# Dummy 64x64 matmuls behind the warm-up, and the retention stretches at other steps of a fused retention and feed-forward kernel

## The chip, the cores and the metric

The kernel runs on one core of one Trainium2 chip. The metric is the device time of one execution in microseconds (us), taken as the median of several runs. TensorE (PE in the profile) does the matmuls; weight loads into its array stand as PEld. VectorE is DVE, ScalarE is ACT, GpSimd is POOL, and SyncE (SP) issues nearly all DMAs.

## The reference

Two stages, one after the other. Shapes: 8 batches, 8 heads, 576 positions, 64 per head; then 4608 tokens, model width 512, inner width 2048.

```python
scores = scale * np.matmul(q, k.transpose(0, 1, 3, 2))
gamma = 1.0 - 2.0 ** (-5.0 - np.arange(H))
rel = pos[:, None] - pos[None, :]
Dmat = np.where(rel >= 0, gamma[:, None, None] ** rel[None], 0.0)
attn = np.matmul(scores * Dmat[None], v)
x = attn.transpose(0, 2, 1, 3).reshape(B * S, H * D)
h = x @ w_in
out = (h - np.tanh(h)) @ w_out
```

## The kernel before, in words

**Tiling.** The 576 positions are cut into nine chunks (n = 0 to 8) of 64. One chunk of all eight batches is a block of 512 tokens. For each block the retention gives x, `mm1(n, f)` computes the f-th of sixteen 128-row pieces of h, and `mm2(n, f)` adds that piece's part of the output into four PSUM banks. Each of mm1 and mm2 is 12 matmuls of 128x128 by 512: every operand is split into a high word and a low word, and three of the four products are kept. In `mm1` the high word of x meets the high word of the weight first, and the low word of the weight is used by the last four matmuls (the first block's f = 0 and 1 have an order of their own).

**Retention.** For each chunk and batch there are three kinds of 64x64 matmul: scores of the chunk, the update of a running state, and the output (`m_score`, `m_state`, `m_out`). They run four at a time on the quarters of the array, in stretches that stand between the large matmuls. `entry` (first two blocks, two batches a time) and `entry3` (later blocks, three stretches for a block: batches 0 and 1, then 2 to 4, then 5 to 7) each are one stretch: the outputs of the batches that are due, their state updates, and last the scores of the batches that follow. In the trace a 64x64 float32 matmul stands as two records.

**Parts of the program.** First a warm-up of bf16 matmuls on zeros (`busy`), then the eight batches of chunk 0 one by one (loop over j; six filler matmuls `busy(6, BLK)` stand in it). Then `seq`: mm1 for blocks 0 and 1, 32 steps k, while the weights are loaded and turned into two words, one piece a step (`unit`, `step`: four operations on DVE at L133, L155, L141, L143, a mask by two on ACT at L100 and L105, and the high word by ACT at L148; L155 makes the low word of the piece before). As no output weight is ready yet, h of these blocks is set aside: in `spill` (in HBM), and for ten pieces first in `home` tiles in SBUF. The stretches `entry` stand at the steps in `early`. Then `late`: mm2 for blocks 1 and 0, 32 steps k, with h fetched back four steps ahead (`fetch`), tanh applied two steps ahead (`resume`), and the words made one step ahead (`words`); the three stretches `entry3` for block 2 stand at three steps k, and four (or two) steps behind each, the q and k for the scores of the next stretch are loaded and scaled (`load_part(rest[0], 0)`, `prep` on POOL). Last the main loop for n = 2 to 8: mm1, mm2 of the piece before, and three stretches at three values of f.

**Order.** `in_order` keeps every engine's instructions in the order of the program, SP's DMA issues too. Who waits for whom follows from tiles: a tile with a `tag` takes one of the tag's slots, and it can be written only when the last instruction that reads the slot's former tile has run, wherever in the program that instruction stands. Tags `wo0` to `wo15` have one slot each and end as the output weights. Before that they hold other things: the first chunk's inputs `a{j}` lie in `wo{15-j}` and are read last by the state update `first_states(b)` that each `entry` carries (`2 * (p - 3)` in the loop, for two batches); the `home` tile of pieces 6 and 7 takes `wo13`, that of 8 and 9 `wo12`, of 11 and 12 `wo11`, of 13 and 14 `wo10`:

```python
home = {0: 7, 1: 7, 6: 13, 7: 13, 8: 12, 9: 12, 11: 11, 12: 11, 13: 10, 14: 10}
loaded[j] = const.tile([P, 3, 4, C], F32, tag=f"wo{NF - 1 - j}", name=f"a{j}")      # load_first
nc.scalar.copy(homes[home[f]][:, (f + 1) % 2 if f > 1 else f], hp)                  # mm1, ACT
```

`pace` makes the weight loads wait for the last copy that ACT made of an h. `scale_k` scales four slices of the first chunk's keys on ACT, `scale_v` the values of a pair of batches on ACT, `scale_q` the queries on DVE.

Of the kernel before, what the change touches and what calls it, by code (L numbers as in the profile page):

```python
# [9 lines left out]
F32 = mybir.dt.float32  # L10
# [7 lines left out]
B, H, S, D = 8, 8, 576, 64  # L18
NT, DM, DF = B * S, H * D, 2048
P = 128  # L20
NF = DF // P
NCC = DM // P
C = 64
NC = S // C
BLK = B * C
# [7 lines left out]
WARM = 24  # L33
# [35 lines left out]
def retention_ffn(ctx: ExitStack, tc: tile.TileContext, ins, out, spill):  # L69
# [5 lines left out]
    psp = ctx.enter_context(tc.tile_pool(name="psp", bufs=1, space=PSUM))  # L75
# [173 lines left out]
    def half(k):  # L249
        return slice(64 * k, 64 * k + 64)  # L250
# [3 lines left out]
    def m_score(j, sc):  # L254
        a = loaded[j]
        return [
            (sc[half(c), i], a[half(c), 1, i, :], a[half(c), 0, i, :], True, True) for i in range(4) for c in range(2)
        ]
# [23 lines left out]
    def run(same, other):  # L282

        while same or other:
            for ms in (same, other):
                for out_, w, x, start, stop in ms[:2]:
                    nc.tensor.matmul(out_, w, x, start=start, stop=stop)  # L287
                del ms[:2]
# [35 lines left out]
    def bank(name, tag):  # L324
        return psp.tile([P, 2, 4, D], F32, tag=tag, bufs=2 if tag == "h" else 1, name=name)
# [5 lines left out]
    def pair(what, j, bank):  # L331
        return what(j, bank[:, 0]) + what(j + 1, bank[:, 1])
# [13 lines left out]
    def entry3(j, later=None):  # L346


        c0, b = divmod(j, B)
        single, states = b > 0, c0 < NC - 1  # L350
        then = j + 2 + single
        o = bank(f"own{j}", "own")
        outs, scores = pair(m_out, j, o), []
        if single:
            two = bank(f"two{j + 2}", "new")
            run(m_score(j + 2, two[:, 1]), outs[:8])
            after_score(j + 2, two[:, 1:], 1)
            outs = outs[8:]
            if states:

                new = bank(f"new{j + 2}", "h")
                run(m_state(j + 2, new[:, 0]), outs[:8])
                outs = outs[8:]
                kept = pool.tile([P, 1, 4, D], F32, tag="cv", bufs=4, name=f"kept{j + 2}")
                nc.scalar.copy(kept, new[:, :1])
        if states:
            new = bank(f"new{j}", "h")
            run(pair(m_state, j, new), outs[:16])
            outs = outs[16:]
        if single:  # L370
            if not states:
                run([], outs)
            outs = m_out(j + 2, two[:, 0], True)
            if states:
                add_state(j, new)
            low = after_out(j, o, 2, False)
        if then < NI:
            sc = bank(f"s{then}", "h")
            scores = pair(m_score, then, sc)
        run(scores, outs)  # L380
        if not single:
            if states:
                add_state(j, new)
            low = after_out(j, o, 2, False)
        low()
        if then < NI:
            after_score(then, sc, 2)
        if single:
            if states:
                add_state(j + 2, kept, 1)  # L390
            after_out(j + 2, two[:, :1], 1)
        def follow():

            more = then % B > 0
            if then >= NI:
                return
            load_part(then, 1)
            prep(then, 1)
            if more:
                load_one(then + 2)  # L400
                prep(then + 2, 1, 1)
                prep(then + 2, 0, 1)
            if later is None:
                load_part(then + 2 + more, 0)
                prep(then + 2 + more, 0)
            else:

                later.append(then + 2 + more)

        if later is None:  # L410
            follow()
        return follow
# [126 lines left out]
    warm = const.tile([P, BLK], BF16, tag="wi15", name="warm")  # L539
    nc.vector.memset(warm, 0.0)  # L540

    wps = psp.tile([P, BLK], F32, tag="new", bufs=1, name="wps")

    def busy(n, cols):
        for _ in range(n):
            nc.tensor.matmul(wps[:, :cols], warm[:, :P], warm[:, :cols], start=True, stop=True)

    busy(WARM, 140)
    busy(8, BLK // 2)
    decay = const.tile([P, 4, C], F32, tag="wo7", name="decay")  # L550
    krows = [const.tile([P, 4, 4, D], F32, tag=f"wo{4 + t}", name=f"krows{t}") for t in range(2)]

# [37 lines left out]
    for j in range(B):  # L590
        o = psp.tile([P, 8, C], F32, tag=("o2", "o3", "own")[j % 3], bufs=1, name=f"own_first{j}")[:, :4]
        run(score_first(j + 2) if j < B - 2 else [], m_out(j, o))
        if j < B - 2:
            after_score(j + 2, firsts[j + 2].unsqueeze(1), 1)
            if 0 < j < 5:
                paced(lambda: upto("load", j + 1))
        if j == 4:
            nc.sync.dma_start(vtab, vtab_d)
            nc.sync.dma_start(krows[0], krows_d[0])
            load_pair(B)  # L600
            nc.sync.dma_start(mask, mask_d)
            upto("load", 7)
            load_pair(B + 2)
        if j == 3:
            busy(6, BLK)
        low = after_out(j, o.unsqueeze(1), 1, False)
        if j == 0:

            paced(lambda: load_paced(6))
        if j < 6:  # L610
            low()
        else:
            lows.append(low)
        if j == 0:
            paced(lambda: load_paced(7))
        if j < 4:
            step()
# [18 lines left out]

    seq = [(n, f) for n in range(2) for f in range(NF)]
    late = [(1, f) for f in turn] + [(0, f) for f in range(NF)]
    early = {5: 4, 8: 5, 10: 6, 14: 7}
    scales = {2: 4, 4: 5, 7: 6, 9: 7, 13: 8}  # L640
    first = 2 * B
    for k, (n, f) in enumerate(seq):
        last_two = k - (len(seq) - 2)
        if k in (2, 6):
            scale_k(k // 4)
        if k + 1 in early:
            scale_v(2 * early[k + 1])
        if last_two < 0:
            step()
        else:  # L650
            fetch(*late[2 + last_two])
        mm1(n, f, ("h", "o2", "h", "o3")[k % 4] if k < len(seq) - 4 else ("o2", "o3", "h", "h")[k % 4])
        if last_two < 0:
            step()
            if k < 24:
                step()
        if k in scales:
            scale_q(2 * scales[k])
        upto("load", k + (7 if k < 11 else 6))
        for at, j, t in ((2, 12, 0), (5, 14, 0), (6, 12, 1), (8, 14, 1)):  # L660
            if k == at:
                load_part(j, t)
        if k in (9, 10):
            load_part(first, k - 9)
        for f in [f for f in home if home[f] == (7, 13, 12, 11, 10)[k - NF]] if NF <= k < NF + 5 else []:
            nc.sync.dma_start(spill[0, f], homes[home[f]][:, (f + 1) % 2 if f > 1 else f])
        if k == 3:
            nc.sync.dma_start(krows[1], krows_d[1])
            behind(tc, pace[-1])
            sc = scores_of(3)  # L670
            ms, done = first_states(0, "new")
            run(pair(m_score, B, sc) + ms, [])
            after_score(B, sc, 2)
            done()
        if k in early:
            p = early[k]
            more = first_states(2 * (p - 3), f"o{(p + 1) % 2}") if p < B - 1 else None
            entry(2 * p, scores_of(p), more)
        if k == 14:
            load_part(first + 2, 0)  # L680
        if k == 26:
            prep(first, 1)
        if k == 28:
            prep(first + 2, 0)
    rest = []
    for k, (n, f) in enumerate(late):
        if k in (3, 16, 29):
            follow = entry3(first + (0, 2, 5)[(3, 16, 29).index(k)], rest)
        if 0 < k < len(late) - 1:
            words(*late[k + 1])  # L690
        if k < len(late) - 2:
            resume(*late[k + 2])
        if k + 4 < len(late):
            fetch(*late[k + 4])
        if k in (3, 16, 29):

            follow()
        if k in (7, 20, 31):
            load_part(rest[0], 0)
            prep(rest.pop(), 0)  # L700
        for _ in range(2 if k < 4 else 1):
            step()
        if k < len(late) - 1:
            mm2(n, f)

    todo = [late[-1]]
    for n in range(2, NC):
        for f in range(NF):
            mm1(n, f)
            todo.append((n, f))  # L710
            if len(todo) > 1 and (n, f) != (NC - 1, NF - 2):
                mm2(*todo.pop(0))
            if n + 1 < NC and f in (2, 6, 14):

                entry3((n + 1) * B + (0, 2, 5)[(2, 6, 14).index(f)])
                mm2(*todo.pop(0))
    mm2(NC - 1, NF - 1)
    in_order(tc)
# [56 lines left out]
```

## Time and profile before

| | |
|---|---|
| median of 3 runs | 882.81 us (882.1 to 883.89) |
| the profiled execution | 883.72 us |
| its span, first to last instruction | 881.9 us |
| mean granted TensorE clock | 0.997 |
| PE busy | 872.7 us |
| DVE busy | 367.3 us |
| ACT busy | 294.4 us |
| POOL busy | 69.4 us |

Busy time is the time in which an engine had at least one instruction at work. Matmuls overlap in the array, so the records of two neighbours overlap too; what counts is the distance between their starts. In a timeline row the columns are the start from the beginning of the span, the time that the merged group took, engine, line, operation, out<-in, shapes, count, and in brackets the idle time of the engine just before with what ended it.

### The profile page before, as it was taken

The page shows a single profiled execution, that of the slowest core. Times are in us where ns is not written, and L with a number is a line of the kernel's source. Part 1 is how long each engine was busy: PE and PEld are TensorE (multiplying, and loading weights), DVE is VectorE, ACT ScalarE, POOL GpSimd, SP SyncE. Part 2 cuts the span into 40 slices and gives each one's busy share as a digit, 9 for nine tenths or more (in the row PEclk, how much of TensorE's full clock was granted, in tenths as well). Part 3 has the DMA queues.
Part 4 walks back from the last instruction along what each step waited for, and adds up shares of the span by engine and source line. Part 5 has one row for each costly group of instructions (what it writes and reads, how often), then busy time and mean ns, then how long its engine had stood idle before and what let it go on. Part 6 is the DMA issues. An engine that isn't in the chain of part 4 may idle for free.

```text
span 881.9 us, 17730 instructions
## 1 busy us (share of the span) xinstructions
PE 872.7 (99%) x7846; PEld 724.3 (82%) x7846; DVE 367.3 (42%) x571; ACT 294.4 (33%) x525; POOL 69.4 (8%) x73
## 2 busy tenths in 40 slices
PE   7999999999999999999999999999999999999997
PEld 6888888888888888888888888888888888888886
DVE  5989876554332333323332433233232332232222
ACT  4887754443222222222222222222222222222222
POOL 0001001011110001101110111001110111000000
PEclk9999999999999999999999999999999999999999
DMA  8966945552410121203220141112120321002001
GB/s 307 374 237 220 367 154 167 142 164 77 116 49 30 49 68 55 78 1 97 73 79 1 50 119 50 30 47 62 62 78 1 97 73 48 1 2 48 1 1 48
DMA packets 37628, 82.06 MB, mean 93 GB/s; under 512 B 4144, under 2 KB 5296, under 8 KB 37552
## 3 DMA queue, kind: packets, MB, share of 16 engines
q1 hardware_dynamic: 37024, 80.02, 28.5%
q8 instruction: 61, 1.00, 0.5%
q10 hardware_dynamic: 528, 0.92, 0.3%
q14 instruction: 15, 0.12, 0.0%
HBM read 63.62 MB, written 17.30 MB: 92 GB/s over the span
## 4 chain that ended last, share of the span: by engine, by line
PE 98%; DMA 1%; ACT 0%; DVE 0%; SPq 0%; issue 0%
PE o L495 45%; PE h L430 45%; PE new L287 2%; PE s L287 2%; PE own L287 2%; PE two L287 1%; DMA rwi<-in_w_in_dram 1%; DMA a<-in_first_dram 1%; PE new_first L287 0%; PE own_first L287 0%; SPq L555 0%; ACT mi L100 0%; ACT xh L313 0%; ACT mi L105 0%; PE s_first L287 0%
## 5 line engine op out<-in xcount | busy, mean ns | idle before, releaser
L430 PE MATMUL h<-xh,wi 128*128 128x512 f32 x1152 | 302.8, 391 | 0.5 <-ACT xh L313 0.5
L495 PE MATMUL o<-wo,gh 128*128 128x512 f32 x1144 | 289.8, 391 | 0.0
L430 PEld LDWEIGHTS h<-xh,wi 128*128 128x128 f32 x1152 | 216.3, 188 | 46.3 <-ACT xh L313 0.7
L495 PEld LDWEIGHTS o<-wo,gh 128*128 128x128 f32 x1144 | 213.1, 188 | 45.0
L456 DVE TENSOR_TENSOR g<-h,g 128x512 f32<-128x512 f32 x114 | 78.8, 691 | 341.5 <-ACT g L455 341.4
L455 ACT ACTIVATE g<-h 128x512 f32<-128x512 f32 x114 | 68.2, 598 | 363.6 <-PE h L430 362.8
L495 PE MATMUL o<-wo,gl 128*128 128x512 f32 x572 | 157.2, 389 | 0.0
L430 PE MATMUL h<-xl,wi 128*128 128x512 f32 x576 | 154.2, 389 | 0.0
L430 PEld LDWEIGHTS h<-xl,wi 128*128 128x128 f32 x576 | 108.1, 188 | 22.6
L495 PEld LDWEIGHTS o<-wo,gl 128*128 128x128 f32 x572 | 107.4, 188 | 22.3
L458 DVE TENSOR_TENSOR gl<-g,gh 128x512 fp32r<-128x512 f32 x113 | 81.0, 717 | 77.6 <-ACT gh L457 72.8
L457 ACT CAST gh<-g 128x512 fp32r<-128x512 f32 x113 | 70.1, 621 | 86.0 <-DVE g L456 86.0
L237 POOL TENSOR_TENSOR vr<-vr,vtab 128x512 f32<-128x512 f32 x21 | 22.4, 1068 | 611.0 <-DMA vr<-in_qkv_dram 525.3
L287 PE MATMUL own<-qk,state 64*64 64x64 f32 x736 | 45.2, 221 | 0.0
L287 PE MATMUL own<-qk,vr 64*64 64x64 f32 x736 | 44.1, 218 | 0.0
L287 PEld LDWEIGHTS own<-qk,vr 64*64 64x64 f32 x736 | 36.8, 135 | 0.0
L287 PEld LDWEIGHTS own<-qk,state 64*64 64x64 f32 x736 | 36.7, 134 | 0.0
L478 DVE TENSOR_TENSOR gl<-s,gh 128x512 fp32r<-128x512 f32 x30 | 23.1, 770 | 24.2 <-PE o L495 13.6
L237 POOL TENSOR_TENSOR qk<-qk,qtab 128x512 f32<-128x512 f32 x20 | 28.4, 1421 | 53.5 <-DMA qk<-in_qkv_dram 53.5
L477 ACT CAST gh<-s 128x512 fp32r<-128x512 f32 x30 | 18.6, 621 | 30.0 <-PE o L495 17.3
L287 PE MATMUL s<-qk 64*64 64x64 f32 x736 | 25.5, 219 | 0.0
L313 ACT CAST xh<-own 128x512 fp32r<-128x512 f32 x25 | 14.7, 586 | 29.9 <-PE own L287 29.9
(85 smaller groups left out, 568.6 us busy)
## 6 DMA issues: line engine op xcount, KB each, us to landing
qk<-in_qkv_dram SPq DMA_DIRECT2D x23, 512.0 KB, 5.9
vr<-in_qkv_dram SPq DMA_DIRECT2D x23, 512.0 KB, 4.5
rwi<-in_w_in_dram SPq DMA_DIRECT2D x16, 512.0 KB, 5.4
rwo<-in_w_out_dram SPq DMA_DIRECT2D x16, 512.0 KB, 5.2
out_dram<-ob SPq DMA_DIRECT2D x61, 128.0 KB, 2.4
s<-spill_dram SPq DMA_DIRECT2D x30, 256.0 KB, 2.7
one<-in_qkv_dram SPq DMA_DIRECT2D x14, 512.0 KB, 5.4
spill_dram<-g SPq DMA_DIRECT2D x20, 256.0 KB, 4.3
```

The source lines that it names most:

```text
L237: nc.gpsimd.tensor_tensor(a, a, table, op=ALU.mult)
L287: nc.tensor.matmul(out_, w, x, start=start, stop=stop)
L313: nc.scalar.copy(xh, o)
L430: nc.tensor.matmul(hp, win[f][:, a, cc, :], x[:, cc, :], start=(k == 0), stop=(k == 3 * NCC - 1))
L455: nc.scalar.activation(g, h, AF.Tanh)
L456: nc.vector.tensor_tensor(g, h, g, op=ALU.subtract)
L457: nc.scalar.copy(gh, g)
L458: nc.vector.tensor_tensor(gl, g, gh.bitcast(F32), op=ALU.subtract)
L477: nc.scalar.copy(gh, g)
L478: nc.vector.tensor_tensor(gl, g, gh.bitcast(F32), op=ALU.subtract)
L495: nc.tensor.matmul(ops[n][t], g[:, t * P : (t + 1) * P], wout[f_][:, a, :], start=(f_ == first and k == 0), stop=(f_ == final and k == 2),)
```

## The change

It alters five things: the warm-up is shorter and has twenty 64x64 float32 matmuls on zeros behind it, in two banks; the six fillers stand one run sooner; and the stretches of 64x64 matmuls stand at other steps in the three parts. In `seq` the first three entries go from steps 5, 8, 10 to 7, 9, 12 (with their `scale_v`, which stands a step ahead) and the second `scale_k` from step 6 to 7. In `late` the stretches go from steps 3, 16, 29 to 16, 22, 28, and the loads behind them from 7, 20, 31 to 20, 26, 31. In the main loop they go from f = 2, 6, 14 to 2, 5, 13.

```diff
-    busy(WARM, 140)
-    busy(8, BLK // 2)
+    busy(WARM, 130)
+    busy(8, 208)
+
+    zeros = warm.bitcast(F32)[:, :C]
+    more = psp.tile([P, 8, C], F32, tag="own", bufs=1, name="wps_own")
+    some = wps.rearrange("p (n c) -> p n c", c=C)
+    run(
+        [(some[half(c), i], zeros[half(c)], zeros[half(c)], True, True) for i in range(6) for c in range(2)],
+        [(more[half(1 - c), i], zeros[half(c)], zeros[half(c)], True, True) for i in range(4) for c in range(2)],
+    )
...
-        if j == 3:
+        if j == 2:
             busy(6, BLK)
...
-    early = {5: 4, 8: 5, 10: 6, 14: 7}
+    early = {7: 4, 9: 5, 12: 6, 14: 7}
...
-        if k in (2, 6):
+        if k in (2, 7):
             scale_k(k // 4)
...
-        if k in (3, 16, 29):
-            follow = entry3(first + (0, 2, 5)[(3, 16, 29).index(k)], rest)
+        if k in (16, 22, 28):
+            follow = entry3(first + (0, 2, 5)[(16, 22, 28).index(k)], rest)
...
-        if k in (7, 20, 31):
+        if k in (20, 26, 31):
             load_part(rest[0], 0)
             prep(rest.pop(), 0)
...
-            if n + 1 < NC and f in (2, 6, 14):
-                entry3((n + 1) * B + (0, 2, 5)[(2, 6, 14).index(f)])
+            if n + 1 < NC and f in (2, 5, 13):
+                entry3((n + 1) * B + (0, 2, 5)[(2, 5, 13).index(f)])
```

More of the change, by code (lines that the diff above doesn't have):

```diff
@@ L694, in retention_ffn @@
             fetch(*late[k + 4])
-        if k in (3, 16, 29):
+        if k in (16, 22, 28):
             follow()
-        if k in (7, 20, 31):
+        if k in (20, 26, 31):
             load_part(rest[0], 0)
```

## The prediction, before the changed kernel was run

> **What bounds the kernel now.** I read the page first, then the waits of PE without the first 18 us, then the chain that ended last, then the stretches around each moved step.
>
> ```profile
> PE 872.7 (99%) x7846; PEld 724.3 (82%) x7846; DVE 367.3 (42%) x571; ACT 294.4 (33%) x525; POOL 69.4 (8%) x73
> PE h L430 <- ACT xh L313: 0.5, 1, 0.5
> 74.29 46.47 PE h L430 x204
> ```
>
> PE is busy for 99% of the span. From 18 us to the end its only wait is the one of 0.5 us shown (the one at 18 us itself). In the chain, 204 large matmuls in a row take 46.47 us, 0.228 us each, so 12 of them (one mm1 or mm2) take 2.73 us. The program is one unbroken row of matmuls: a stretch that moves without a wait costs and gains nothing, and a wait that appears on PE is lost in full. So each moved step is asked one thing: are its inputs there when PE arrives?
>
> The only time to be won lies ahead of 18 us and just behind it:
>
> ```profile
> 8.56 0.63 ACT mi L105
> 9.94 5.31 DMA a<-in_first_dram
> 18.03 12.35 PE h L430 x48
> ...
> 6.60:10.00 3.40, 2.13 (x91) 1.77 (x89) 1.79 (x5) 1.81 (x4) 0.00 (x0) 1.00 1.02 400
> 13.40:16.80 3.40, 1.78 (x70) 1.45 (x64) 1.79 (x5) 1.24 (x4) 0.00 (x0) 1.00 0.95 372
> 16.90:20.20 3.30, 2.83 (x19) 2.26 (x16) 2.76 (x8) 2.54 (x8) 0.00 (x0) 0.50 0.97 330
> ```
>
> The first three rows are of the chain, the others of busy time by stretch (the first figure behind the length is PE's, the last but two the granted clock). The chain into mm1 is ACT's mask of the first weight at 8.56, behind it a load of first inputs that is issued at 9.94 and lands at 15.25, then the last runs of the first chunk and their copy by ACT. PE's own pace is no link of it before 15 us. From 16.9 to 20.2 the clock is granted at 0.50. There 48 matmuls take 12.35 us where 48 x 0.228 = 10.94: the dip costs some 1.4 us at most.
>
> **The change, part by part.**
>
> *Warm-up, dummies, fillers.* 24 x 10 + 8 x 48 = 624 columns of 5408 go, and 20 matmuls (40 records) come.
>
> ```profile
> 1.19 4.69 PE L546 MATMUL wps<-warm 128*128 128x140 bf16 x32 [1.19 <-DVE warm L540]
> 5.81 1.03 PE L287 MATMUL s_first<-a 64*64 64x64 f32 x16
> ```
>
> 4.69 us x 624 / 5408 = 0.54 us saved. Sixteen records of one list take 0.8 us from first to last start there, so 24 records with 16 more beside them in the other list take about 1.2. The first scores start some 0.7 us later. The load issued at 9.94 covers it, for what it waited behind is ACT's mask at 8.56 and not PE; without that cover it would cost 0.7. The fillers add nothing, one run sooner: what is behind them still waits for the landing at 15.25. I take 0 for all of it; the ends are -1.4 (the clock dip goes) and +0.7.
>
> *`early`, 5 to 7.* This step meets a slot. `home` of piece 6 takes `wo13` at step 6. `a2` lies there, and its last reader is the state update in the first entry. Before, that entry stood at step 5. Now it stands at step 7, so the copy of piece 6 on ACT waits for a stretch that PE reaches only after mm1 of piece 7. ACT keeps its order, and behind that copy stand the mask, the high word of weight piece 8, the four slices of `scale_k` (now at 7), and the copy and high word of the next step.
>
> ```profile
> 37.99 0.27 PE L287 MATMUL s<-qk 64*64 64x64 f32 x2
> 39.91 1.10 PE L287 MATMUL new_first<-a,krows 64*64 64x64 f32 x32
> 40.94 1.19 PE L430 MATMUL h<-xh,wi 128*128 128x512 f32 x4
> ...
> 40.51 0.58 ACT L313 CAST xh<-own 128x512 fp32r<-128x512 f32 x1
> 41.54 1.71 ACT L630 ACTIVATE krows<-krows,vtab 128x256 f32<-128x256 f32 x4
> 43.99 0.59 ACT L435 COPY home<-h 128x512 f32<-128x512 f32 x1 [0.74 <-PE h L430]
> 45.73 0.60 ACT L148 CAST wi<-mi 128x512 fp32r<-128x512 f32 x1
> 46.24 1.28 ACT L247 ACTIVATE vr<-vr,vtab 128x128 f32<-128x128 f32 x4
> ...
> 41.12 0.69 DVE L315 TENSOR_TENSOR xl<-own,xh 128x512 fp32r<-128x512 f32 x1 [0.57 <-ACT xh L313]
> 45.86 0.69 DVE L133 SCALAR_TENSOR_TENSOR mi<-rwi,mi 128x512 int32<-128x512 int32 x1 [0.92 <-ACT mi L105]
> 46.47 0.68 DVE L155 TENSOR_TENSOR wi<-mi,wi 128x512 fp32r<-128x512 f32 x1
> 47.78 0.69 DVE L143 SCALAR_TENSOR_TENSOR mi<-rwi,mi 128x512 int32<-128x512 int32 x1
> 48.40 0.68 DVE L242 TENSOR_TENSOR early<-early,qtab 128x512 f32<-128x512 f32 x1
> ```
>
> These are timeline rows of PE, ACT and DVE around the entry at step 5. On PE the entry starts at 37.99, half of its last 32 records (those of `a2`) end about 2.56 later, and mm1 follows 2.95 after the entry's start. In the new order two more mm1 come first: the entry starts at 37.99 + 2 x 2.72 = 43.43, `a2` is free at 45.99, and mm1 of piece 8 could start at 46.38.
>
> First wait. ACT's copy of piece 6 starts at about 46.1. The high word starts 45.73 - 43.99 = 1.74 behind that copy and takes 0.60, so it is ready at 48.44. PE waits 2.1 us. Before, the same word was ready at 46.33, about when PE came, so there is no spare time to swallow this.
>
> Second wait. ACT goes on 0.51 after the high word's start (46.24 - 45.73), at 48.35. It does the four slices (1.71, of which 0.06 overlap), the copy of piece 7 at 50.0 and the high word of piece 9 at 51.74, ready at 52.34. PE is through with mm1 of piece 8 at 48.5 + 2.72 = 51.2. It waits 1.2 us. Without `scale_k` there it would not wait; in the old order `scale_k` lay ahead of the copy.
>
> Third wait. DVE was stopped too, at L133, which waits for the mask. It makes the low word of piece 8 at 48.58 (0.14 after the high word, as 46.47 against 46.33), starts L143 1.31 later, L242 at 50.5, and the entry's three operations: the first at 51.1, then L315 behind ACT's xh (0.51 after 51.74, 0.58 long, so 52.95), L329 0.61 later (the pitch of 45.86 and 46.47), L133 at 54.17, and L155, the low word of piece 9, at 54.78, ready at 55.46. mm1 of piece 9 started at 52.4 and needs it for its last four matmuls, 8 x 0.227 later, at 54.2. It waits 1.3 us.
>
> Then the entry at 9 gives PE 2.95 us of other work, ACT and DVE catch up, and I find no further wait up to step 14. Sum 2.1 + 1.2 + 1.3 = 4.6 us. Ends: 2.1 if ACT's and DVE's queues recover at once, 6 if a fourth wait of about 1 us follows at pieces 11 to 13. The loads of weights 12 and 13 are held on SP by the same copies, by one step; they are used four steps on, and I take 0 for that. The `scale_v` that comes with the entry stands ahead of a copy that waits anyway: 0.
>
> *`late`.* The first stretch at 16 has its inputs long since. The loads behind it now stand at 20 and the stretch that uses them at 22: two mm2 between, where there were nine.
>
> ```profile
> 130.88 0.50 PE L495 MATMUL o<-wo,gh 128*128 128x512 f32 x1
> 169.42 2.11 PE L495 MATMUL o<-wo,gh 128*128 128x512 f32 x8
> 185.88 1.98 PE L495 MATMUL o<-wo,gh 128*128 128x512 f32 x8
> 166.47 0.27 PE L287 MATMUL two<-one 64*64 64x64 f32 x2
> 168.38 0.22 PE L287 MATMUL s<-qk 64*64 64x64 f32 x2
> ...
> 145.43 0.43 SPq L209 DMA_DIRECT2D qk<-in_qkv_dram  x1
> 174.84 8.41 SPq L465 DMA_DIRECT2D s<-spill_dram  x4
> 183.78 0.42 SPq L209 DMA_DIRECT2D qk<-in_qkv_dram  x1
> 149.58 1.30 POOL L237 TENSOR_TENSOR qk<-qk,qtab 128x512 f32<-128x512 f32 x1 [6.54 <-DMA qk<-in_qkv_dram]
> 188.53 1.29 POOL L237 TENSOR_TENSOR qk<-qk,qtab 128x512 f32<-128x512 f32 x1 [7.62 <-DMA qk<-in_qkv_dram]
> ```
>
> Count from the mm2 behind a stretch (130.88 for the old step 3, 169.42 for the old step 16). The mm2 six steps on starts 16.46 later (185.88), so the next stretch, which comes ahead of it, starts at +16.5, and its scores come 168.38 - 166.47 = 1.91 into it, at +18.4. The q and k for them are issued four steps behind the first stretch. SP is late there, for it issues the fetches of h in order, and those waited for data that landed late beside the two large loads of the stretch: the row of four fetches takes 8.41 us. Issue was at +14.55 (145.43) and +14.36 (183.78), and POOL ended scaling at 150.88, +20.0, and at 189.82, +20.4. PE needs it at +18.4. So the stretch at 22 (which repeats the old step 3, with the same loads) waits 1.5 us, and the one at 28 (which repeats the old step 16) waits 2.0. Sum 3.5 us. The lower end is 0, if the fetches recover within four steps; the upper 4.5, if the load takes a microsecond longer. I take 3.5, as both rows say so. The last loads, at 31, follow the third stretch as before. That the first stretch leaves the steps in which weights are still being converted gains 0, for PE had no wait there.
>
> *Main loop.* Between f = 2 and 5 lie 6 x 2.73 = 16.4 us where 21.8 lay.
>
> ```profile
> 231.98 0.50 PE L495 MATMUL o<-wo,gh 128*128 128x512 f32 x1
> 240.52 1.69 POOL L237 TENSOR_TENSOR qk<-qk,qtab 128x512 f32<-128x512 f32 x1
> ```
>
> The last input is ready at 242.21, 10.2 us behind the mm2 at 231.98. 6 us of cover are left, so 0; without the cover, each of the six blocks would lose what is short. From 13 to the next 2 it is longer than before.
>
> **Sum.** 0 + 4.6 + 3.5 + 0 = 8.1 us. On the profiled execution (883.72) that is 891.8; the median (882.81) lies 0.9 below it, and gives 890.9. I say 891.0.
>
> **Rivals.**
>
> *The clock falls in a new wait.* In the row 13.40:16.80 PE was busy 1.78 of 3.40 us and the clock was at 0.50 in the next stretch; at 2.13 of 3.40 (6.60:10.00) it stayed. A wait of 2.0 to 2.1 us that falls whole into such a stretch leaves 1.4 busy. A fall costs half of 3.4, 1.7 us. Behind the early waits most of that is covered, for PE then waits less for ACT; in `late` it is lost. One fall: 892.6; two: 894.3. Against it: the waits are 1.2 and 1.5 elsewhere, and a wait may be split between two stretches.
>
> The Trainium skill, "TensorE: Matmul & The Clock Gate" (Part 1, the table of states, and the closing table), states that the clock is halved after an idle window of about 3.4 us and that gaps under about 3 us are safe. By that rule no wait here halves it and 890.9 stands; by the rows above a half-idle stretch is enough. The dip at 16.9 agrees with the rows.
>
> *Only one of the two waits is real.* If the fetches recover, 882.8 + 4.6 = 887.4; if ACT's queue does not matter, 882.8 + 3.5 = 886.3.
>
> *Faster.* Neither wait shows, and the fillers one run sooner, with the dummies, keep PE busy enough in the stretch 13.40:16.80 that the dip at 16.9 does not come: 882.8 - 1.1 = 881.7. This decides if the waits are together under 1.1 us. For it speaks the moved work; against it the slot of `a2`, which is in the code.
>
> *The moves do nothing:* 882.8, if all waits are hidden and the dip stays.
>
> **How the numbers follow.** Both waits, clock kept: 0.36 (890.9). Both, with a fall: 0.26 (892.6 to 894.3). Early wait alone 0.14, late wait alone 0.07, more than 895 0.03. Faster 0.09, within 0.2% (1.8 us, about what this measurement can tell from no change) 0.05. So slower 0.86. The range 885.5 to 894.5 leaves out the last three cases and a bit of the second.
>
> **What would show it.** In the profile after: a wait of ACT at L435 for PE at about 43 to 46 us; PE waits at L430 for ACT or DVE of about 2, 1 and 1 us between 46 and 56; two PE waits at L287 (`s`) for POOL of 1.5 to 2 us in `late`; none in the main loop. The prediction is wrong if ACT copies piece 6 before the first entry, if the fetches run on time behind the stretch at 16, or if 18 us comes much earlier.

## The result, and the profile after

The changed kernel takes 894.5 us (median of four runs, 892.73 to 896.79) where the kernel before takes 882.61 beside it: ratio 1.0134, interval 1.0107 to 1.0161. It is 11.9 us slower. The prediction was 891.0 with 885.5 to 894.5. The profiled execution is the fastest of the four, 892.73 us, with a span of 890.9 against 881.9 before; what the trace can explain is therefore 9.0 us. One execution of a later kernel, the profiled one with the edges back, ran at a granted clock of 0.655 and took 1248.6 us; it is left out of that kernel's times.

First the page of the kernel after: its first line, and PE's share.

```profile
span 890.9 us, 17803 instructions
PE 873.8 (98%) x7886; PEld 723.4 (81%) x7886; DVE 367.3 (41%) x571; ACT 294.3 (33%) x525; POOL 68.6 (8%) x73
```

PE's busy time is what it was (872.7 before; 40 more matmuls). The span has grown by waits alone. These are PE's waits of the kernel after from 18 us on (us in total, times, the longest), where the kernel before had one of 0.5:

```profile
PE h L430 <- ACT wi L148: 3.4, 3, 1.9
PE s L287 <- POOL qk L237: 2.3, 2, 1.3
PE o L495 <- ACT gh L477: 1.5, 2, 0.9
PE h L430 <- DVE wi L155: 0.9, 1, 0.9
```

These are idle times; where the text goes by the distance between starts, a wait is 0.1 to 0.2 us longer. The last row and 2.8 us of the first belong to `early`, the two between to `late`; 0.6 us of the first stands at 23.8 us, ahead of both. The timeline of the kernel after, ACT's, DVE's and PE's rows, shows the first group:

```profile
45.36 0.58 ACT L435 COPY home<-h 128x512 f32<-128x512 f32 x1 [4.43 <-PE new_first L287]
47.08 0.60 ACT L148 CAST wi<-mi 128x512 fp32r<-128x512 f32 x1
47.58 1.71 ACT L638 ACTIVATE krows<-krows,vtab 128x256 f32<-128x256 f32 x4
49.19 0.56 ACT L435 COPY home<-h 128x512 f32<-128x512 f32 x1
50.90 0.60 ACT L148 CAST wi<-mi 128x512 fp32r<-128x512 f32 x1
...
53.83 0.68 DVE L155 TENSOR_TENSOR wi<-mi,wi 128x512 fp32r<-128x512 f32 x1
...
47.73 1.20 PE L430 MATMUL h<-xh,wi 128*128 128x512 f32 x4 [1.95 <-ACT wi L148]
51.56 1.20 PE L430 MATMUL h<-xh,wi 128*128 128x512 f32 x4 [0.81 <-ACT wi L148]
54.56 1.20 PE L430 MATMUL h<-xh,wi 128*128 128x512 f32 x4 [0.90 <-DVE wi L155]
```

ACT stands idle for 4.43 us in front of the copy of piece 6, until the entry's state update (`new_first`) has read `a2`. Everything behind that copy is late: the word of piece 8 ends at 47.68 and PE starts at 47.73; the word of piece 9 ends at 51.50, PE starts at 51.56; DVE's low word ends at 54.51, PE starts at 54.56.

The second group, SP's, POOL's and ACT's rows of the same timeline:

```profile
174.57 1.54 SPq L209 DMA_DIRECT2D vr<-in_qkv_dram  x1
176.17 0.51 SPq L223 DMA_DIRECT2D one<-in_qkv_dram  x1
176.77 10.22 SPq L465 DMA_DIRECT2D s<-spill_dram  x4
187.04 0.43 SPq L209 DMA_DIRECT2D qk<-in_qkv_dram  x1
190.94 1.27 POOL L237 TENSOR_TENSOR qk<-qk,qtab 128x512 f32<-128x512 f32 x1 [6.34 <-DMA qk<-in_qkv_dram]
211.77 1.27 POOL L237 TENSOR_TENSOR qk<-qk,qtab 128x512 f32<-128x512 f32 x1 [7.68 <-DMA qk<-in_qkv_dram]
185.30 0.62 ACT L477 CAST gh<-s 128x512 fp32r<-128x512 f32 x1 [0.81 <-DVE s L471]
...
131.46 0.62 ACT L148 CAST wo<-mo 128x512 fp32r<-128x512 f32 x1 [2.17 <-DVE mo L143]
131.99 0.61 ACT L477 CAST gh<-s 128x512 fp32r<-128x512 f32 x1
135.37 0.62 ACT L148 CAST wo<-mo 128x512 fp32r<-128x512 f32 x1 [2.24 <-DVE mo L143]
135.90 0.61 ACT L477 CAST gh<-s 128x512 fp32r<-128x512 f32 x1
```

POOL has scaled q at 192.21 and 213.04; PE's scores start at 192.26 and 213.09, having waited 1.4 and 1.25 us by the distance between starts. That is the mechanism of the prediction: q is issued at 187.04, behind four fetches that take SP 10.22 us. The last five rows were not in it. `gh` comes late three times: at 132.60 and 136.51, behind ACT's conversion of a weight which itself waits for DVE (PE loses 0.3 and 1.1 us, by starts), and at 185.92 (0.8 us), when the fetched h has come in behind the loads of 174.57 and 176.17.

One more place is of use, the stretch in which the clock was at 0.50 before (busy time by stretch, kernel after; the last but two is the granted clock):

```profile
16.90:20.20 3.30, 2.98 (x13) 2.47 (x14) 2.86 (x9) 3.15 (x8) 0.00 (x0) 1.00 0.99 368
```

The dip is gone, and so is the wait of 1.2 us at 14.68 that the kernel before had in its first scores; in its stead PE waits 1.1 us for a first input at 14.83. The first mm1 starts at 17.22 (18.03 before). But a wait for ACT comes at 23.8 (0.6 us idle, 0.8 by starts), and the row of matmuls up to the first entry takes 12.31 us as it took 12.28. The entry is reached at 29.53, 0.8 us sooner.

### The profile page after: what moved, and what is told of

Its sections match the earlier page's. It is cut to its first block, busy times and chain, and to the rows that moved or that the text cites. A ratio compares the mean times of both kernels' runs of the same rounds, so it can differ in the third digit from the quotient of the medians.

```text
span 890.9 us, 17803 instructions
## 1 busy us (share of the span) xinstructions
PE 873.8 (98%) x7886; PEld 723.4 (81%) x7886; DVE 367.3 (41%) x571; ACT 294.3 (33%) x525; POOL 68.6 (8%) x73
## 4 chain that ended last, share of the span: by engine, by line
PE 91%; DMA 4%; DVE 3%; ACT 2%; issue 1%; POOL 0%; SPq 0%; ACTq 0%; POOLq 0%; DVEq 0%
PE h L430 43%; PE o L495 40%; PE s L287 2%; PE new L287 2%; PE own L287 1%; DMA s<-spill_dram 1%; PE two L287 1%; DMA qk<-in_qkv_dram 1%; DMA rwi<-in_w_in_dram 1%; DVE s L471 1%; DVE gl L478 1%; DMA a<-in_first_dram 1%; PE new_first L287 0%; ACT gh L477 0%; POOL qk L237 0%
## 5 line engine op out<-in xcount | busy, mean ns | idle before, releaser
L287 PE MATMUL own<-qk,state 64*64 64x64 f32 x736 | 45.2, 221 | 0.0
L287 PE MATMUL own<-qk,vr 64*64 64x64 f32 x736 | 44.1, 218 | 0.0
L287 PEld LDWEIGHTS own<-qk,vr 64*64 64x64 f32 x736 | 36.8, 135 | 0.0
L287 PEld LDWEIGHTS own<-qk,state 64*64 64x64 f32 x736 | 36.7, 134 | 0.0
L478 DVE TENSOR_TENSOR gl<-s,gh 128x512 fp32r<-128x512 f32 x30 | 21.1, 703 | 25.1 <-PE o L495 12.6
L287 PE MATMUL s<-qk 64*64 64x64 f32 x736 | 25.6, 219 | 2.3 <-POOL qk L237 2.3
L287 PEld LDWEIGHTS s<-qk 64*64 64x64 f32 x736 | 23.3, 135 | 4.0 <-POOL qk L237 2.6
```

Of the source, the lines that this page charges most:

```text
L478: nc.vector.tensor_tensor(gl, g, gh.bitcast(F32), op=ALU.subtract)
```

## The experiments

Every kernel was timed against the kernel before on the same chip; the kernel before had medians of 882.64 to 882.94 there.

### The four parts, each alone

The diff cut into four: the start (warm-up, dummies, fillers), `early` with `scale_k`, `late`, and the main loop, each put into the kernel before.

> The kernel before with the start of the change alone: shorter warm-up, twenty dummies, fillers one run sooner. Theory: in the changed kernel's profile the first mm1 began at 17.2 instead of 18.0 us and the clock did not fall at 17 us, but a wait of 0.8 us for a weight's high word gave part of it back. So 0.8 us less, 881.8 us, with mm1 beginning at 17.2 and no PE wait on an instruction fetch inside the first runs. Rival, the start is hidden behind the first loads, as the prediction had it: 882.6 us and mm1 at 18.0.

> The kernel before with the entries of the first part at 7, 9, 12 and the second scale of keys at 7, nothing else. Theory: ACT's copy of piece 6 waits for the slot of a2 and PE waits 2.1, 1.0 and 1.1 us at pieces 8 and 9: 4.2 us more, 886.8 us. Rival, the waits of the changed kernel there come from its earlier start (PE ahead of the weights): under 2 us more, 884.5 us.

> The kernel before with the stretches of the second part at 16, 22, 28 and the loads at 20, 26, 31, nothing else. Theory: PE waits for POOL's scaled q in the stretches at 22 and 28 (2.7 us together) and, without a stretch at 3, for the words of h near steps 3 and 4 and at 21 (2.1 us together): 4.8 us more, 887.4 us. Rival, only the two waits for q are of this edit, and the others came with the later clock of the first part: 2.7 to 3.5 us more, 885.7 us.

> The kernel before with the stretches of the main loop at f = 2, 5, 13, nothing else. Theory: 6 us of cover stay, no wait: 882.6 us, within 0.3 us. Rival, part of what the changed kernel lost came from the closer stretches in six blocks: some 2 us more.

| part alone | us | ratio, interval | the prediction's term |
|---|---|---|---|
| start | 899.57 | 1.0193, 1.0178 to 1.0208 | 0 |
| `early`, `scale_k` | 888.32 | 1.0072, 1.0055 to 1.0089 | 4.6 |
| `late` | 889.85 | 1.0086, 1.007 to 1.0101 | 3.5 |
| main loop | 883.23 | 1.0004, 0.9994 to 1.0013 | 0 |

`early` and `late` came out above what was expected of them, 886.8 and 887.4. The surprise is the first row. The start alone costs 16.7 us, more than the whole change, and the four together (16.7 + 5.5 + 7.0 + 0.4 = 29.6) are two and a half times what the change costs. The parts don't add. PE's waits from 18 us on, of the start alone:

```profile
PE new_first L287 <- issue: 4.2, 2, 3.6
PE two L287 <- issue: 4.2, 4, 1.2
PE s L287 <- issue: 2.1, 2, 1.1
PE o L495 <- issue: 1.6, 2, 1.2
```

The same of `early` alone:

```profile
PE new_first L287 <- issue: 3.1, 2, 2.2
PE h L430 <- ACT wi L148: 1.0, 2, 0.6
PE h L430 <- DVE wi L155: 0.9, 1, 0.9
```

So `early` alone is no measure of the term of 4.6: 3.1 us of its waits are of another kind, and the one of 2.2 us stands in the first entry behind the last read of `a2`, so that the word of piece 8, ready at 46.72, comes in while PE waits there until 46.75. The slot holds ACT's copy as before (4.40 us). The first two of `late` alone:

```profile
PE s L287 <- POOL qk L237: 4.3, 2, 3.1
PE o L495 <- ACT gh L477: 1.3, 2, 0.9
```

Here the waits for q are longer than the 1.5 and 2.0 us of the prediction (the longest 3.1). "issue" is a wait for nothing that the profile names: no semaphore, no data. With the start alone it stands inside stretches of 64x64 matmuls, all through the main loop, where not one line was changed. The largest one (3.6 us at 63.3) also lets the clock fall: in these two stretches of busy time PE is busy for 0.10 of 3.40 us, and then runs at 0.51.

```profile
59.60:63.00 3.40, 0.10 (x2) 0.00 (x0) 2.83 (x6) 0.92 (x2) 0.00 (x0) 0.99 0.99 308
62.95:66.40 3.45, 3.11 (x30) 2.70 (x30) 1.38 (x3) 1.39 (x3) 0.00 (x0) 0.51 0.46 179
```

In the trace, each of these waits for "issue" ends 1.2 to 1.6 us after a packet of 16,384 bytes on queue 8, which the page calls "instruction". So PE waited for its own code. Counting PE's records in the trace from the start (a wide matmul has two, its weight load and itself; a 64x64 matmul has four; the waits of PE's sequencer count too, some 70 in all), with the first record as 0, PE resumes at these numbers:

```
kernel                PE resumes at  record  mod 256  since the edge before  code packet
start alone              39.37 us     1216     192        2.80 us            36.86-37.96
start alone              63.29 us     1984     192        5.78 us            60.23-61.75
start alone             174.97 us     3776     192        3.15 us           172.38-173.53
start alone             504.19 us     9920     192        3.00 us           501.87-502.74
early alone              46.74 us     1216     192        4.63 us            44.24-45.24
early alone              69.85 us     1984     192        3.27 us            67.45-68.43
kernel before            14.68 us      449     193                           12.03-13.23
```

In all kernels of this study every wait behind 18 us that has no named releaser and ended in this way behind such a packet (31 of at least 0.5 us of PE or PEld) ended at a record that is 192 or 193 modulo 256. The code comes in blocks of 256 instructions, and the waits stand at the edges of blocks. Theory A is then: the 20 dummies are 80 instructions, they move every edge behind them by 80 (the shortened warm-up has as many matmuls as before), and edges that lay in harmless places now lie where PE runs a block through in 3 us, which only a stretch of 64x64 matmuls can do. In the change as a whole the other parts move the stretches too, and no edge hits. The rivals: the dummies' own PSUM tiles or the fillers' place do it (B), or every further instruction costs something (C).

### The start alone, with the edges back

Twelve dummies and 8 warm-up matmuls of 512 columns, 64 PE instructions as before, in place of 20 dummies and 32 matmuls:

```
-    busy(WARM, 130)
-    busy(8, 208)
+    busy(8, BLK)
...
-    ... for i in range(6) for c in range(2)],
-    ... for i in range(4) for c in range(2)],
+    ... for i in range(4) for c in range(2)],
+    ... for i in range(2) for c in range(2)],
```

> The start part alone again (dummy 64x64 matmuls and fillers one run sooner), but with 12 dummies and 8 warm-up matmuls of 512 columns, 16 + 48 = 64 PE instructions where the kernel before has 32 x 2 = 64, so that nothing behind them lies at another place in PE's instruction stream. Theory A (block edges: PE's code comes in blocks of 256 instructions, in every trace so far PE's waits for code end at the instruction whose number is 192 modulo 256, and 80 more instructions push these edges into the 64x64 stretches): the waits of the start part alone (0.9 us at 39.4, 3.8 at 63.3, 1.3 at 175, some 1.2 in each item of the main loop, its 16.7 us in all) are gone; 881.5 to 884 us. Rival B (the dummies' PSUM tiles or the fillers' new place cost the time): it stays above 895 us. Rival C (more instructions as such, by what they add to fetch): as A here, but then the next run, whose edges are moved without a dummy, would not tell apart from it; it is the place of the waits that does.

Measured 882.3 us against 882.64, ratio 0.9997 (0.9988 to 1.0006). The 16.7 us are gone, with dummies and moved fillers in place: B falls. This rests on the time alone; no list of waits is shown for this kernel. The start part itself is worth nothing.

### The edges moved, nothing else

```
-    busy(WARM, 140)
+    busy(WARM + 40, 52)
```

> The kernel before with nothing changed but its first 24 warm-up matmuls of 140 columns cut into 64 of 52: 40 more matmuls of no use, 80 more PE instructions, no dummy, no moved filler, no moved stretch. Theory A (block edges): PE waits for code inside the same stretches as with the start part alone, at instruction numbers 192 modulo 256, 0.7 to 1.4 us each at some 11 places and more where the clock falls after one; 895 to 901 us. Rival B (the dummies or the fillers are what costs): 882 to 884 us. Counted on the times between instructions in the trace of before, an edge moved by 80 would be reached in under 3.2 us after the one ahead of it at 11 places (12.99 us in all against that figure), by 0 to 16 at none.

Measured 900.3 us, ratio 1.0198 (1.0181 to 1.0215), with neither dummies nor a moved stretch. PE's waits in it, from 18 us on:

```profile
PE new_first L287 <- issue: 4.2, 2, 3.6
PE two L287 <- issue: 3.9, 4, 1.2
PE s L287 <- issue: 1.6, 2, 0.9
PE o L495 <- issue: 1.4, 2, 1.2
```

Line for line the waits of the start alone, at the same places (40.92, 64.82, 176.10, then 407.72 to 701.21), all at 193 modulo 256. Between two such edges lie 2.8 to 3.3 us in the main loop: the code packet starts 0.6 to 0.9 us after the earlier edge, takes 0.9 to 1.3, and PE resumes 1.2 to 1.6 us after it. Theory A is shown.

The Trainium skill, "Runtime: NRT & Kernel Launch" (Instruction fetch mechanics), says that code is refilled in 16 KiB blocks of 256 instructions, which the sequencer fetches while it executes the current one, and that crossing a boundary is mostly hidden. The trace agrees on the blocks (packets of 16,384 bytes, 61 of them in the kernel before); hidden it is only where the packet is in before PE is through with the block ahead.

### Is the fifth part of the shift a fifth of the cost?

```
-    busy(8, BLK)          (of the kernel with the edges back)
+    busy(16, BLK // 2)
```

> The start part alone with 12 dummies and 16 warm-up matmuls of 256 columns in place of 8 of 512: 16 PE instructions more than the kernel before. Theory A (block edges): counted on the times between instructions in the trace of before, edges moved by 16 meet no stretch that runs a block through in under 3.2 us; no wait for code behind 20 us, 881.5 to 884 us. Rival (every instruction more costs, in proportion): a fifth of the 16.7 us of 80, so 885.5 to 886.5 us.

Measured 884.67 us, ratio 1.0019 (1.0009 to 1.0029). A miss for both: I had counted on no wait. Its only waits for code:

```profile
41.72 1.09 PE L430 MATMUL h<-xl,wi 128*128 128x512 f32 x4 [1.09 <-issue]
64.22 0.63 PE L430 MATMUL h<-xl,wi 128*128 128x512 f32 x2 [1.87 <-issue]
```

Both are at 193 modulo 256, just behind a stretch, 4.70 and 5.90 us after the edge before; the main loop has none. Here the code packet started 2.4 and 3.7 us after the edge, not 0.6 to 0.9. Up to 75 us the DMA engines are busy with weights (page of the kernel after: the first slices are at 0.5 to 0.9). So the bound of 3.2 us held in the main loop and was too low in the front, where these waits ended up to 5.9 us behind the edge before. That the DMA traffic is what delays the packet was not tried by itself. Nor is the time between edges all: in the kernel with the main loop's move alone PE runs a whole block in 1.86 us (edges at 248.79 and 250.65; five more blocks up to 489 us take 1.86 or 1.87) without a wait, as its code packet started at 245.81, 3.0 us ahead of the first of these edges. That edge lies a few records inside the stretch, so the packet started while PE was still at wide matmuls; how far ahead it is asked for was not measured.

### The main loop's move, in the kernel after

```
-            if n + 1 < NC and f in (2, 5, 13):
+            if n + 1 < NC and f in (2, 6, 14):
```

> The kernel after, with the stretches of the main loop back at f = 2, 6, 14. Theory A (block edges): the move to 2, 5, 13, worth nothing in the kernel before (883.23 us against 882.86), is what keeps the edges moved by the 80 instructions out of the main loop's stretches; without it the waits for code of the start part alone come back from 400 us on (0.9, 1.4, 1.1, 1.4, 1.3, 1.2, 1.2 us at seven stretches), so 900 to 904 us. Rival B (the main loop's move is worth nothing in either kernel): 894 to 895.5 us.

Measured 903.72 us, 9.2 more than the kernel after. Its waits for code:

```profile
PE two L287 <- issue: 3.8, 3, 1.5
PE s L287 <- issue: 3.0, 2, 1.6
PE o L495 <- issue: 1.2, 1, 1.2
```

8.0 us, from 463 us on, each at 193 modulo 256. (This list is of the slowest of its four runs, 906.9 us, in which the waits for q are 4.0 us in place of 2.3 and the clock fell three times; it can't be added up to the 9.2 us of the medians.) The same edit is worth nothing in the kernel before and 9 us in the kernel after. This is what joins the parts.

### `early` without the slot

Pieces 6 and 7 lose their home in `wo13`:

```
-    home = {0: 7, 1: 7, 6: 13, 7: 13, 8: 12, 9: 12, ...
+    home = {0: 7, 1: 7, 8: 12, 9: 12, ...
```

> The kernel after, without a home for the pieces 6 and 7 of x (their copies no longer wait for the slot wo13 of a2; they go the way of the pieces that have no home). Theory: the wait for the slot is what holds the pieces' high words at 47.7 and 51.6 us, 2.0 + 1.0 us of PE, and part of the 1.1 us at 54.6 us; without it 890.5 to 892 us. Rival (the two home copies and the words are late because ACT and DVE have too much to do there, not for the slot): 894 to 895 us, the gaps at 47.7 and 51.6 us stay.

Measured 888.39 us, ratio 1.0061 (1.0047 to 1.0075), 2 us below what was expected, 6.1 less than the kernel after by the medians, 4.9 by the spans. PE's waits, from 18 us on:

```profile
PE s L287 <- POOL qk L237: 2.7, 2, 1.4
PE o L495 <- ACT gh L477: 1.4, 2, 0.9
PE h L430 <- ACT wi L148: 0.6, 1, 0.6
```

All three waits between 46 and 56 us are gone (the 0.6 left is that at 23 us). From the first mm1 to the matmul behind the entry at step 14, PE needs 56.10 us where the kernel after needs 60.64 and the kernel before 56.19. In this count the slot costs 4.5 us, and the rest of `early` nothing.

### `late`: the loads sooner, or the first stretch back

```
-        if k in (20, 26, 31):        -  k in (16, 22, 28)  ...  k in (20, 26, 31)
+        if k in (17, 23, 31):        +  k in (3, 22, 28)   ...  k in (7, 26, 31)
```

> The kernel after, with the loads for the second and third late stretch at steps 17 and 23 in place of 20 and 26. Theory: q for the scores is scaled too late (waits of 1.4 and 1.25 us at 192 and 213 us) because its rows are asked for too late, so both waits go and the gh wait of 0.8 us at 186 us, which is put down to fetches queued behind these loads, moves some 8 us earlier with them: 891.5 to 892.5 us. Rival (GpSimd is late on its own account, whatever the rows do): the waits stay, 894 to 895 us.

> The kernel after, with the first late stretch back at step 3 and its load at step 7 (stretches at 3, 22, 28, loads at 7, 26, 31). Theory: the stretch at step 3 is cover for ACT and DVE, which without it hand gh over 0.3 and 1.1 us late at 132.7 and 136.6 us, and the load at 20 is what delays gh at 186 us (0.8 us) and q at 192 us (1.4 us); all four go and the wait at 213 us (1.25 us) stays: 890.5 to 891.5 us. Rival (the conversions are late for another reason, and late's cost is all in q): only the wait at 192 us goes, 893 us.

Loads sooner: 891.97 us, ratio 1.0104 (1.0089 to 1.012). The waits for POOL are gone from its list; the wait for `gh` at 186 us stayed (0.6 us) and didn't move, for the loads, asked for at 17, left SP at 175.10 in place of 174.57: two output stores ahead of them hold the queue. At 211.6 us there is a new wait of 0.7 us for "issue", at no edge (record 4371, 19 modulo 256), and one of 0.5 for DVE behind it; the cause of the first is open. First stretch back at 3: 891.83 us (889.73 to 893.0), ratio 1.0105 (1.0087 to 1.0123), just above the expected range. Its waits, from 18 us on:

```profile
PE h L430 <- ACT wi L148: 2.6, 2, 1.9
PE s L287 <- POOL qk L237: 2.2, 1, 2.2
PE h L430 <- DVE wi L155: 0.4, 1, 0.4
```

`gh` is no longer in the list, and one wait for q is left, as expected; that one is 2.2 us and not 1.25. `early` is short of one wait in this list because the clock fell behind its first one (see below). The stretch at step 3 was cover for ACT and DVE, which still convert weights there. Why the q wait grew was not followed up: its q was issued at 203.55 and landed at 208.73.

### Both bills taken away

No home for pieces 6 and 7, late stretches at 3, 22, 28, loads at 7, 25, 31; dummies, fillers, `early` and the main loop as in the kernel after.

> The kernel after with both bills taken away: no home for the pieces 6 and 7, late stretches at 3, 22, 28 with loads at 7, 25, 31. Theory: 888.4 us (no home for these pieces) less the late part's 5.1 us of waits (0.3, 1.1, 0.7, 1.5, 1.6 in its trace, the last one all but gone with the load a step sooner), so 883 to 884.5 us, the time of the kernel before: the start and the main loop have nothing to give. Rival (the start part saves 0.8 us or more that the waits hide): below 882 us.

Measured 883.07 us against 882.94, ratio 1.0006 (0.9996 to 1.0015). Its only wait from 18 us on is one that the kernel after has too, at 23 us:

```profile
PE h L430 <- ACT wi L148: 0.6, 1, 0.6
```

So the change comes apart, by medians: the slot 6.1 us (894.5 to 888.39), the late steps 5.3 (888.39 to 883.07), all else 0.1. No version beat the kernel before, and nothing in the traces points to one: its only wait for code, at 14.68, is gone in the kernel with both bills away, where PE reaches the first mm1 at 16.34 and gives 0.8 us (by starts) of that back at 23.4.

## Why the prediction was right, and where not

The sign and the size came out: 891.0 said, 894.5 measured, at the edge of the range.

`early`: right in mechanism and size. Predicted: ACT's copy at 46.1 (45.4 measured, the start being 0.8 sooner), waits of 2.1, 1.2 and 1.3 us; the rows of the kernel after have 1.95, 0.81 and 0.90 of idle time, which is 2.0, 1.0 and 1.1 by the distance between starts. The sum of 4.6 measured 4.5 by the kernel without the slot.

`late`: the waits for q were right in place and cause, 1.5 and 2.0 said (the first is 1.6 by its own rows, 20.0 less 18.4), 1.4 and 1.25 measured. Their size is not fixed: in kernels whose late part is the same, the idle time for q is 2.3 us (kernel after), 2.7 (without the slot) and 4.0 (main loop back). The term was too small, because of one sentence: "That the first stretch leaves the steps in which weights are still being converted gains 0, for PE had no wait there." No gain was right, but it had hidden a loss. PE had no wait there *because* the stretch gave ACT and DVE two microseconds (128.85 to 130.88 in the kernel before); without it `gh` is late by 0.3 and 1.1 us, and by 0.8 more at 186 us behind the loads. 3.5 us measured 4.6 (spans) to 5.3 (medians).

Start: 0 said, and the kernel with the edges back gives 0 (0.9997). The dip of the clock, priced at 1.4 us at most, went, and the row of matmuls it stood in took 12.31 us as before 12.28, for a wait for ACT came in its place. But the step left out what 80 more instructions do to code that is not touched, and that term runs from 0 to 16.7 us, beyond any end given (-1.4 to +0.7). That it came out as 0 in the changed kernel was luck of where the edges fell: the same for "Main loop: 0", which is right in the kernel before and worth 9 us in the company of the start. The two errors cancel. The trace of before could have shown it: its wait `PE s_first L287 <- issue` of 1.2 us at 14.68 ends at record 449, behind a code packet.

The clock did not fall in any of the new waits of the profiled execution (mean granted clock 0.999). Nor does a fall make the median: the two runs about it, 893.7 and 895.3 us, had 1.000 and 0.999; the slowest, 896.79, had 0.994, and a fall there can't be ruled out. But the mechanism of this rival is real. In three later kernels with the same first wait of 1.95 us (main loop back, loads sooner, first late stretch back) the clock was at 0.50 for 3.41 us behind it. These are the stretches of the last:

```profile
44.54:47.95 3.41, 1.46 (x22) 1.19 (x19) 1.47 (x3) 3.28 (x7) 0.00 (x0) 1.00 0.48 165
47.95:51.36 3.41, 3.41 (x10) 2.64 (x9) 2.38 (x5) 3.38 (x8) 0.00 (x0) 0.50 0.76 260
```

PE is busy for 1.46 of 3.41 us, the 1.4 that the rival asks for. The second wait of `early` is then gone and the third is 0.4 us in place of 0.9, as the rival says too, so a fall there costs nothing: from the end of the first wait to the next entry PE needs 8.0 us with it (47.01 to 54.97) as in the kernel after without (47.73 to 55.70). In the kernel after, the wait was split between two such stretches, with 2.39 and 2.48 us busy (43.39:46.80 and 46.80:50.21): where it fell was luck. Over all traces but that with the edges back, nine stretches of 3.41 us with PE busy for under 1.8 us were followed by a clock of 0.50 and two were not (1.44 and 1.62 us, late alone and first late stretch back); with 1.9 us or more none was. So a half-idle stretch was mostly enough, as the prediction's rows have it, and the other rule that it sets beside them does not hold here.

The rivals with one wait only, the faster one, and "the moves do nothing" are out by the list of waits.

Open: the profiled execution accounts for 9.0 us. The median run was 1.8 us longer than it (894.5 against 892.73); which of the waits grew in the others is not known; the waits for q, which differ most between traces, could have.

## What to carry to other kernels

Where PE is the bound and its code is unrolled, adding or taking away instructions anywhere ahead moves the 256-instruction edges of all code behind; test an insertion against a kernel with the same count of useless instructions before its own merits are judged, and keep the count when only the content is to change. Parts of such a change don't add up, so undo them singly in the whole as well as doing them singly. And a stretch on the bounding engine is cover for the others: ask what it hides before it is moved, even where no wait is seen.

## What was not expected of the hardware

- PE waits for its own code at edges of 256 instructions, where it gets through the block before the next one's packet is in: such waits ended 2.8 to 3.6 us behind the edge before from 170 us on and up to 5.9 us in the front, and took up to 3.6 us each. Where the packet had started 3 us ahead, a block of 1.86 us cost nothing. 80 useless instructions at the start cost 17.7 us of 882.6.
- The clock fell to 0.50 behind a wait of 1.95 us, in three traces with PE busy for 1.46 or 1.47 of the 3.41 us before, and not in the kernel after, where the same wait was split between two stretches.
- From the end of the code packet to PE's next instruction there are 1.2 to 1.6 us, in every one of these waits.
- The same edit can be worth 0.4 us (main loop, in the kernel before; the interval includes 0) or 9.2 us (in the kernel after), by where the edges lie.
